# Loads that wait for their product of TensorE in the program, not in the plan alone

## The chip, the cores and the metric

The kernel runs on one core of a Trainium2 chip. The metric is the device time of one execution in microseconds (us); less is better. Engines are called as the profile calls them: PE (TensorE, matrix products), DVE (VectorE), ACT (ScalarE), POOL (GpSimd, which here only issues the row gathers), SP (SyncE, which here only issues loads and stores), and the 16 DMA engines that carry out what POOL and SP issue.

## The reference

Two branches work on the same x of 2048 tokens by 576, and a gate mixes them:

```python
g = sigmoid((x * gate_w).sum(-1))
a = irfft2(rfft2(x) * (w_r + 1j * w_i))          # branch A: a filter in the frequency domain
q = einsum("nd,dhc->nhc", x, w_q)                # branch B: 32 heads, two halves of 128 each
s1, s2 = q1 @ k1.T, q2 @ k2.T                    # 64 scores for each half
e = argmax(s1) * 64 + argmax(s2)                 # one expert of 4096 for each token and head
act = gelu(einsum("nd,nhd->nh", x, u[e]))
b = einsum("nh,nh,nhd->nd", softmax_over_one, act, v[e])
out = g * a + (1 - g) * b
```

All is float32. Every token reads 32 rows of u and v, 2 x 576 numbers each, from memory: 65,536 rows of 4,608 bytes, 302 MB in all.

## The kernel before, in words

The 2048 tokens are 16 tiles of 128. The 32 heads are 8 chunks (c = 0 to 7) of 4 heads. The work has two stages that overlap.

**Scores and experts (to about 585 us).** For each chunk, the key tables are first multiplied into the query weights: `build_m` takes five slices of w_q (i = 0 to 4, tiles `wqT` and `wq`, loaded by `load_wq` at L361 and L364 into a slot of the ring "uv") and makes a matrix of two parts, `mh` and `ml`. `scores(c, tp)` then multiplies two token tiles (tp = 0 to 7) with the five slices: a *score block*, written (c, tp) below, of ten jobs on PE (two tiles by five slices), 28 matmuls in all. The first job of a block, `score_jobs[c, tp][0]`, has three matmuls. DVE takes the maxima (`mx`, L446), ACT the signs (`sg`, L454), and a few operations later the experts' numbers stand in `ei`.

**Gathers and sums (all along, to the end).** `group(t, c)` fetches the rows of one token tile and one chunk: four gathers by POOL (L519), one a head, 128 rows of 4,608 bytes each, into slots of the ring "uv". DVE multiplies them with x and sums (L529), ACT applies the gelu (L533), and the second half of the row is added to the output, either by DVE (L561, or ACT L554 and DVE L555) or as a product with a diagonal matrix on PE (ACT makes `dg` at L571, PE accumulates, DVE adds at L587). Token tiles 0 to 9 are summed beside the scores; tiles 10 to 15 (`L_SEQ`) after them, and their x is loaded for this a second time (`xl`, by `load_xn`, L382).

**The frequency branch (from about 600 us).** `fold` adds and subtracts mirrored columns of x (DVE, L694 to L696) and PE multiplies with `kr`; `f2`, `f4`, `f6` and `invert` are products with tables: `fi` (loaded at L684), twiddle factors `tw` (L725) and the filter `w` (L732). `close_gates` makes the gate's sums from `xl` at L393.

**What sets the order.** Nothing is issued as it is written. Each operation is a job with an engine, a cost in us, a due time and the buffers it needs; `Plan.order` simulates engines, buffers and DMA by these costs and so fixes the order of the jobs on each engine and the buffer slots. The kernel then emits the jobs in that order. Along one engine a chain of dependencies without semaphores keeps the order (`after`, `on`). Between engines, semaphores come from the data alone: an instruction waits for what wrote its inputs and for what last used its buffer.

A job can also be given `after=[...]`: jobs that the plan lets end before it starts this one. It is a hint for the plan's clock. In the program it has no trace, unless the data ask for the same wait. Three kinds of loads have one:

- `load_wq` for slice i of chunk c+1: after the first job of the score block two before the block at which the slice is built (`BUILD`; none for the very first): 34 loads. The build itself is planned after the first job of the block just before.
- `load_xn` for the six `xl` tiles: after the first job of block (7, 7), the last.
- the load of `fi`: after the same job.

So 41 loads of the 120 DMAs that SP issues. (POOL's gathers have such an `after` too; the change does not touch them.)

The order of SP's queue around block (7, 7) is: `kr`, `gr`, `krb`, the six `xl`, `fi`, then the first `w` and `tw`, then the second `w` and `tw`, and so on. SP issues in order; one that waits holds all behind it.

Of the kernel before, what the change touches and what calls it, by code (L numbers as in the profile page):

```python
# [82 lines left out]


class Job:
    __slots__ = ("eng", "us", "at", "fn", "deps", "bufs", "move", "nr", "wait", "outs", "ready", "start", "end", "table")


REACH = {'POOL': 3.72, 'SP': 1.95}
# [167 lines left out]
def tile_kernel(ctx, tc, xn, xT, x5, wqT, wq5, kT, wri, uv, gw, t_kr, t_fi, t_tw, t_io, out):  # L257
# [13 lines left out]
    prev = {}  # L271

    def after(chain, i):
        if chain in prev:
            tc.add_manual_dep(
                i.ins, prev[chain].ins.name,
                mybir.DependencyInfo(mybir.DependencyClass.NoSync, mybir.DependencyReason.DATA),
                reason="order of the work")
        prev[chain] = i
# [19 lines left out]
    plan = Plan(sizes)  # L299
# [20 lines left out]
    def on(eng, i):  # L320
        after(eng, i)
# [8 lines left out]
    def ac(us, at, fn, w, r, **kw):  # L330
        return plan("ACT", us, at, lambda: on("ACT", fn()), w, r, **kw)

    def ld(us, at, fn, w, r=(), **kw):
        return plan("SP", 0.06, at, lambda: on("SP", fn()), w, r, move=us, **kw)

    vt, stt, actv = nc.vector.tensor_tensor, nc.vector.scalar_tensor_tensor, nc.scalar.activation
    pp = pools["pp"]
# [20 lines left out]
    def load_wq(c, i, at, after=()):  # L358
        w = wq_t[c, i] = buf("uv", ROW, view=lambda x: x.rearrange("p a d -> p (a d)")[:, : 8 * P].rearrange("p (g e) -> p g e", g=8))
        if i < 4:  # L360
            ld(load(P * 4096, 4096), at, lambda: nc.sync.dma_start(w.ap, wqT[c, i]), [w], after=after)  # L361
            return
        flat = lambda: w.ap.rearrange("p g e -> p (g e)")[:, 512:]
        ld(load(P * 2048, 2048), at, lambda: nc.sync.dma_start(flat(), wq5[c]), [w], after=after)  # L364
        ac(act(512), at + 2, lambda: actv(w.ap[:, :, :E], flat().rearrange("p (g e) -> p g e", e=E), AF.Copy), [w], [])
        ac(act(512), at + 2, lambda: actv(w.ap[:, :, E:], w.ap[:, :, :E], AF.Copy), [w], [])

    def load_x(b, i, at, at2, n=1):
        st = buf("uv", ROW, view=lambda x: x.rearrange("p a d -> p (a d)")[:, : n * 512])
        h = P if i < 4 else E  # L370
        src = lambda: xT[:, i, b * 512 : (b + n) * 512] if i < 4 else x5[:, b * 512 : (b + n) * 512]
        ld(load(h * n * 2048, n * 2048), at, lambda: nc.sync.dma_start(st.ap[:h], src()), [st])
        for m in range(n):
            hi = xts[i if i < 4 else 8][b + m]
            lo, r = (xts[4 + i][b + m], 0) if i < 4 else (hi, E)
            cut = lambda m=m: st.ap[:h, m * 512 : m * 512 + 512]
            ac(act(512), at2, lambda hi=hi, cut=cut: actv(hi.ap[:h], cut(), AF.Copy), [hi], [st])
            dv(dve(512), at2, lambda hi=hi, lo=lo, cut=cut: vt(lo.ap[r : r + h], cut(), hi.ap[:h].bitcast(F32), ALU.subtract), [lo], [st, hi])
# [245 lines left out]
    for s in range(NCH * 8):  # L624
        c, tp = divmod(s, 8)
        at = when(s)
# [17 lines left out]
        while todo and todo[0][0] * 8 / NE + LE <= s + 1:  # L644
            n, (t, cc) = todo[0]
            ready = t // 2 if cc == 0 and t // 2 < EARLY else t // 4 * 2 + 1
# [21 lines left out]
    def switch(m):  # L668
        sctx[m].close()
        pools[("la", "lb")[m]] = ctx.enter_context(  # L670
            tc.tile_pool(name=("la", "lb")[m], bufs=1, side=("right", "left")[m], reuse_waits="tile"))
# [223 lines left out]
    for n, t in enumerate(E_T + L_SEQ):  # L895
        at = inv0 + IPACE * n
# [5 lines left out]
    for n, (t, c) in enumerate(SEQ):  # L902
        at = TR + TGS * n
# [11 lines left out]
    for j in plan.order():  # L915
        for m in range(2):
            if not opened[m] and j.start >= plan.switch[m]:
                opened[m] = True
                switch(m)
        tc.cur_priority = int(j.start * 100) + 1000  # L920
        for b in j.bufs:
            if b.ap is None:
                b.ap = b.make(b.tag, b.slot)
        j.fn()


EARLY = 4
# [82 lines left out]
```

## Time and profile before

| | |
|---|---|
| time, median of 3 runs | 965.13 us (962.98 to 965.76) |
| the profiled execution: its own time | 973.46 us |
| its span, first to last instruction | 971.7 us |
| PE busy | 914.7 us (94%) |
| DVE busy | 878.6 us (90%) |
| ACT busy | 622.4 us (64%) |
| POOL busy | 566.0 us (58%) |
| DMA: the gathers' queue q0 | 302.02 MB, 82.0% of the 16 engines' span |
| DMA: SP's queue q1 | 41.94 MB, 11.8% |
| mean granted clock of PE | 0.984 |

How to read it: busy shares are means over the whole run, and two engines and the DMA are all above 90%. So what a change is worth can't be read from them; it is read from the stretch in which it acts, by what each engine waits for there. A profiled execution is one run, and this one was longer than the median of the timed ones; sums made from its rows are set against its own time.

### The profile page before, as it was taken

To read this page: it belongs to the slowest core of one execution; us is meant where nothing else is said; L and a number is where in the kernel's file an instruction comes from. 1 tells how busy PE (TensorE), PEld (TensorE's weight loads), DVE (VectorE), ACT (ScalarE), POOL (GpSimd) and SP (SyncE) were. 2 spreads that over 40 slices of the span, in tenths; PEclk is the share of its full clock that TensorE was granted. 3 is DMA by queue.
4 is the path that set the end of the run, shared out by engine and by line. 5 is a ranking of instruction groups with operands and counts; after the bars stand their busy time and mean duration, and the time that the engine had idled before them with its cause. 6 is when DMAs were issued, how large, how long until landed. Compare 5 with 4: busy or idle time off the path is not lost.

```text
span 971.7 us, 14880 instructions
## 1 busy us (share of the span) xinstructions
PE 914.7 (94%) x4288; PEld 747.3 (77%) x4288; DVE 878.6 (90%) x2030; ACT 622.4 (64%) x2211; POOL 566.0 (58%) x516
## 2 busy tenths in 40 slices
PE   7999999999999999999999993799999999999994
PEld 7888888788788888777878782787788787777763
DVE  3899989999999999999999889998999999967687
ACT  3987786977676776876788865664344444654443
POOL 0346666665565565565666656477674647756662
PEclk9999999999999999999999997899999999999997
DMA  9889999999998999899999998799998989999995
GB/s 325 276 283 406 356 327 371 318 378 362 343 356 334 342 379 342 318 372 379 333 350 378 389 420 325 298 347 413 418 385 331 401 292 390 378 391 379 409 367 238
DMA packets 90897, 344.90 MB, mean 355 GB/s; under 512 B 10240, under 2 KB 10752, under 8 KB 90816
## 3 DMA queue, kind: packets, MB, share of 16 engines
q0 software_dynamic: 73728, 302.02, 82.0%
q1 hardware_dynamic: 17088, 41.94, 11.8%
q8 instruction: 34, 0.56, 0.2%
q14 instruction: 47, 0.39, 0.1%
HBM read 339.20 MB, written 4.72 MB: 354 GB/s over the span
## 4 chain that ended last, share of the span: by engine, by line
PE 65%; DVE 16%; ACT 8%; issue 5%; DMA 4%; POOL 1%; another core or an unknown queue 0%; SPq 0%; DVEq 0%; POOLq 0%; ACTq 0%
PE p L318 65%; DVE uv L529 5%; DMA uv<-uv,ei 3%; ACT sg L454 3%; DVE xn L561 3%; DVE xn L555 2%; ACT uv L554 2%; DVE mx L446 1%; POOL uv L519 1%; ACT a L538 1%; ACT dg L571 1%; DMA uv<-wqT 1%; DVE t L753 0%; DVE t L752 0%; DVE sq L470 0%
## 5 line engine op out<-in xcount | busy, mean ns | idle before, releaser
L519 POOL DMA_INDIRECT uv<-uv,ei x512 | 565.8, 1105 | 389.2 <-PE p L318 110.4
L318 PE MATMUL p<-mh,xt 128*128 128x512 f32 x1152 | 383.6, 400 | 3.1 <-issue 1.7
L454 ACT ACTIVATE sg<-p,mx 128x64 bf16<-128x64 f32 x1024 | 231.3, 375 | 48.7 <-DVE mx L446 39.6
L318 PEld LDWEIGHTS p<-mh,xt 128*128 128x128 f32 x1152 | 216.5, 188 | 53.2 <-issue 1.9
L318 PE MATMUL p<-ml,xt 128*128 128x512 f32 x640 | 251.9, 394 | 0.0
L529 DVE SCALAR_TENSOR_TENSOR uv<-uv,xn 128x576 f32<-128x576 f32 x320 | 234.3, 749 | 6.6 <-DMA uv<-uv,ei 6.1
L318 PE MATMUL p<-uv,dg 128*128 128x288 f32 x800 | 209.8, 416 | 23.9 <-ACT dg L571 22.4
L318 PEld LDWEIGHTS p<-uv,dg 128*128 128x128 f32 x800 | 152.9, 194 | 70.7 <-ACT dg L571 26.8
L318 PEld LDWEIGHTS p<-ml,xt 128*128 128x128 f32 x640 | 120.4, 188 | 27.1
L529 DVE SCALAR_TENSOR_TENSOR uv<-uv,xl 128x576 f32<-128x576 f32 x192 | 138.6, 750 | 0.4 <-issue 0.3
L561 DVE SCALAR_TENSOR_TENSOR xn<-uv,a,xn 128x576 f32<-128x576 f32 x152 | 122.6, 809 | 0.9 <-issue 0.2
L533 ACT ACTIVATE b<-z 128x4 f32<-128x4 f32 x129 | 28.7, 223 | 141.0 <-DVE uv L529 103.7
L555 DVE TENSOR_TENSOR xn<-uv,xn 128x576 f32<-128x576 f32 x148 | 111.2, 752 | 3.1 <-ACT uv L554 1.3
L554 ACT ACTIVATE uv<-uv,a 128x576 f32<-128x576 f32 x148 | 104.7, 777 | 13.1 <-DVE a L542 9.8
L318 PE MATMUL p<-fi,bt 128*128 128x289 f32 x384 | 99.0, 411 | 3.6 <-DVE t L753 2.3
L318 PEld LDWEIGHTS p<-fi,bt 128*128 128x128 f32 x384 | 83.4, 243 | 17.0 <-issue 4.2
L318 PEld LDWEIGHTS p<-kT,uv 128*128 128x128 f32 x640 | 78.1, 195 | 8.8 <-issue 4.9
L318 PE MATMUL p<-kT,uv 128*128 128x128 f32 x640 | 78.9, 279 | 5.4 <-DMA uv<-wqT 4.9
L446 DVE TENSOR_REDUCE mx<-p 128x16 f32<-128x1024 f32 x64 | 77.8, 1216 | 6.1 <-PE p L318 6.0
L465 ACT ACTIVATE sg<-sg 128x256 bf16<-128x256 bf16 x192 | 79.2, 463 | 0.9
L571 ACT ACTIVATE dg<-ident,a 128x128 f32<-128x128 f32 x200 | 69.4, 409 | 2.5 <-PE p L318 2.4
L538 ACT ACTIVATE a<-b,sw 128x1 f32<-128x1 f32 x200 | 43.4, 305 | 1.0
(97 smaller groups left out, 708.4 us busy)
## 6 DMA issues: line engine op xcount, KB each, us to landing
uv<-wqT SPq DMA_DIRECT2D x32, 512.0 KB
uv<-uv,ei POOLq DMA_INDIRECT x512
w<-wri SPq DMA_DIRECT2D x16, 289.0 KB
out<-xn SPq DMA_DIRECT2D x16, 288.0 KB
xn<-xn SPq DMA_DIRECT2D x10, 288.0 KB
tw<-t_tw SPq DMA_DIRECT2D x9, 256.0 KB
uv<-xT SPq DMA_DIRECT2D x8, 256.0 KB
uv<-wq SPq DMA_DIRECT2D x8, 256.0 KB
```

The lines of the kernel that those rows point to most:

```text
L318: after("PE", nc.tensor.matmul(*args, **kw))
L446: dv(dve(1024, True), at + O_MAX, lambda: nc.vector.tensor_reduce(mv.ap[:, 2 * tp : 2 * tp + 2, :], ps.ap.rearrange("p a (g e) -> p a g e" ...
L454: on("ACT", actv(sg.ap[:, j, g, :], ps.ap[:, j, g * E : g * E + E], AF.Sign, bias=mv.ap[:, 2 * tp + j, g : g + 1], scale=-1.0))
L465: ac(act(256), at + O_ADD, lambda b=b: actv(s2()[:, :, b * Q : b * Q + Q], s2()[:, :, b * Q : b * Q + Q], AF.Copy, bias=b / 4), [sg], [])
L519: on("POOL", nc.gpsimd.indirect_dma_start(out=g.ap.rearrange("p a d -> p (a d)"), out_offset=None, in_=uv, in_offset=bass.IndirectOffsetOn ...
L529: dv(0.68, at + O_DOT, lambda k=k, g=rows[k]: stt(g.ap[:, 0, :], g.ap[:, 0, :], 1.0, x.ap, op0=ALU.mult, op1=ALU.mult, accum_out=z.ap[:, k ...
L533: ac(0.1, at + O_GELU, lambda: actv(b.ap[:, k0:k1], z.ap[:, k0:k1], AF.Gelu_apprx_tanh), [b], zk, table="gelu")
L538: on("ACT", actv(a.ap[:, k : k + 1], b.ap[:, k : k + 1], AF.Copy, scale=sw[:, t, c * HPC + k : c * HPC + k + 1]))
L554: ac(act(576), at + O_SCALE, lambda v=v, s=s: actv(v(), v(), AF.Copy, scale=s()), [(rows[k], 1)], [a])
L555: dv(dve(576), at + O_SUM, lambda v=v: vt(y.ap, v(), y.ap, ALU.add), [y], [(rows[k], 1)])
L561: dv(0.73, at + O_SUM, lambda v=v, s=s: stt(y.ap, v(), s(), y.ap, op0=ALU.mult, op1=ALU.add), [y], [(rows[k], 1), a])
L571: ac(0.3, at + O_DG, lambda k=k, dg=dg: actv(dg.ap, ident, AF.Copy, scale=a.ap[:, k : k + 1]), [dg], [a, "ident"])
```

## The change

Each load's `after` is now also put into the program. When a load is emitted, a dependency with a semaphore is added on the last instruction of each job that it names. To know that instruction, the last matmul of every PE job is kept in the job (`last`) when the job is emitted. The plan, its order on each engine and the buffer slots stay the same, and no DMA is added or taken away.

```diff
-    __slots__ = (..., "start", "end", "table")
+    __slots__ = (..., "start", "end", "table", "last")
...
-    def ld(us, at, fn, w, r=(), **kw):
-        return plan("SP", 0.06, at, lambda: on("SP", fn()), w, r, move=us, **kw)
+    def ld(us, at, fn, w, r=(), after=()):
+        def go():
+            i = fn()
+            on("SP", i)
+            for j in after:
+                tc.add_manual_dep(
+                    i.ins, j.last.ins.name,
+                    mybir.DependencyInfo(mybir.DependencyClass.Sync, mybir.DependencyReason.DATA),
+                    reason="not before its turn")
+
+        return plan("SP", 0.06, at, go, w, r, move=us, after=after)
...
         j.fn()
+        if j.eng == "PE":
+            j.last = prev["PE"]
```

More of the change, by code (lines that the diff above doesn't have):

```diff
@@ L85 @@
 class Job:
-    __slots__ = ("eng", "us", "at", "fn", "deps", "bufs", "move", "nr", "wait", "outs", "ready", "start", "end", "table")
+    __slots__ = ("eng", "us", "at", "fn", "deps", "bufs", "move", "nr", "wait", "outs", "ready", "start", "end", "table", "last")
 REACH = {'POOL': 3.72, 'SP': 1.95}
```

## The prediction

> **What bounds the kernel now.** I read the page first, then the busy time by stretches, the waits of TensorE (PE) by stretches, and the chain that ended last.
>
> ```profile
> span 971.7 us, 14880 instructions
> 540.00:560.00 20.00, 20.00 (x87) 15.93 (x85) 14.74 (x35) 16.31 (x75) 14.34 (x14) 1.00 1.01 385
> 560.00:580.00 20.00, 20.00 (x89) 16.37 (x88) 17.69 (x41) 11.49 (x46) 10.88 (x11) 1.00 1.03 420
> 580.00:600.00 20.00, 10.28 (x36) 7.42 (x34) 18.70 (x43) 12.84 (x58) 11.18 (x10) 0.83 0.85 329
> 600.00:620.00 20.00, 12.01 (x78) 11.58 (x79) 18.50 (x54) 11.49 (x36) 10.21 (x10) 0.74 0.95 370
> 620.00:640.00 20.00, 16.62 (x95) 14.51 (x94) 19.49 (x56) 14.16 (x55) 11.29 (x10) 0.91 0.72 238
> 640.00:660.00 20.00, 20.00 (x94) 17.36 (x93) 16.40 (x46) 13.15 (x33) 15.59 (x14) 1.00 1.00 391
> ```
>
> The columns after the length are PE, PE's weight loads, VectorE (DVE), ScalarE (ACT), GpSimd (POOL), PE's granted clock, the busy share of the DMA engines, GB/s. PE is full up to 580 and from 640. Between them it loses 21 us (60 less 10.28, 12.01 and 16.62), while DVE is nearly full. Just before, from 540 to 580, it is the other way round: the DMA engines are full (1.01, 1.03) and DVE has holes.
>
> The waits of PE, in the stretches 60 to 500 (three lines, all there are) and 577 to 640 (the two longest of four); the numbers are us in total, times, longest:
>
> ```profile
> PE p L318 <- ACT dg L571: 2.5, 2, 1.3
> PE p L318 <- issue: 1.7, 1, 1.7
> PE p L318 <- ACT sg L454: 1.1, 2, 0.8
> ...
> PE p L318 <- DVE f L695: 9.3, 3, 7.6
> PE p L318 <- ACT dg L571: 8.6, 2, 7.7
> ```
>
> Up to 500 PE hardly waits (5.3 us), so there only what makes PE itself late can cost. In 577 to 640 it waits 17.9 us for folds and diagonals that DVE and ACT deliver late. The chain that ended last tells why they are late:
>
> ```profile
> 490.70 6.72 DMA uv<-uv,ei
> ...
> 506.67 46.69 PE p L318 x196
> ...
> 559.21 14.40 DMA uv<-uv,ei
> ...
> 586.31 1.15 DVE mx L446
> ```
>
> PE carries the chain until 553; then a gather of rows that takes 14.40 us from issue to landing, where 6.72 was usual; then DVE, which works off what came late, reaches the row maxima (mx) at 586.31. ACT's signs and diagonals come behind these, and PE, whose row stands in the next fence, resumes at 592.14 behind the diagonals.
>
> **The change, part by part.** 41 loads carry an `after`: 34 of the key product's weights (L361, L364), six of x (xl, L382) and fi (L684). For each, SyncE (SP) now waits until the last matmul of the named score product is done. No transfer is added or removed; what moves is when SP issues, and what stands behind it in SP's queue.
>
> *The seven held behind the first product of the last score block, (7, 7).* Here are SP's issues, PE's matmuls, and the sizes:
>
> ```profile
> 526.55 27.10 SPq L382 DMA_DIRECT2D xl<-xn  x6
> 553.74 0.38 SPq L684 DMA_DIRECT2D fi<-t_fi  x1
> 554.17 0.42 SPq L732 DMA_DIRECT2D w<-wri  x1
> 554.65 0.42 SPq L725 DMA_DIRECT2D tw<-t_tw  x1
> ...
> 578.40 0.61 PE L318 MATMUL p<-mh,xt 128*128 128x512 f32 x2
> 584.07 0.39 PE L318 MATMUL p<-ml,xt 128*128 128x512 f32 x1
> 592.14 5.83 PE L318 MATMUL p<-uv,dg 128*128 128x288 f32 x16 [7.68 <-ACT dg L571]
> ...
> xl<-xn SPq DMA_DIRECT2D x6, 288.0 KB
> fi<-t_fi SPq DMA_DIRECT2D x1, 867.0 KB
> w<-wri SPq DMA_DIRECT2D x16, 289.0 KB
> tw<-t_tw SPq DMA_DIRECT2D x9, 256.0 KB
> ...
> q1 hardware_dynamic: 17088, 41.94, 11.8%
> ```
>
> The last score block ends with the matmul at 584.07. A block is 28 matmuls, some 0.23 us apart, so it begins 6.4 us before its end, and the first of the pair at 578.40 is the third matmul of its first product: done at about 578.8. Today the six xl loads go out from 526.55 to 553.65 and fi at 553.74. They will go out from 578.8 on: 25 to 52 us later. Behind them in SP's queue stand one load of w and one of tw (554.17, 554.65), which carry no `after` but move as well, by 24 us. In all 6 x 288 + 867 + 289 + 256 = 3140 KB, 3.2 MB. Queue q1 takes 11.8% of 971.7 us for 41.94 MB, 2.73 us for a MB: 8.8 us of all DMA engines leave the stretch 526 to 570, where the engines are full, and come back after 579.
>
> What it brings before 579 is bounded by what DVE loses there to late rows:
>
> ```profile
> DVE uv L529 <- DMA uv<-uv,ei: 3.7, 4, 1.4
> DVE mx L446 <- PE p L318: 2.5, 1, 2.5
> DVE uv L529 <- issue: 0.2, 1, 0.2
> ```
>
> These are all the waits of DVE from 553 to 577. The 2.5 us for PE stay, and come first, at 551 to 553; so DVE can gain 3.7 + 0.2 = 3.9 us behind them, and no more, though the rows may come 8.8 us sooner. I take 3.9 whole, because 8.8 is more than twice that. From 575 to 596 DVE has no hole, so it reaches mx at 582.4 in place of 586.31 (the scores that it reads are there at 578), ACT's diagonals follow, and PE resumes at 588.2: its wait of 7.68 becomes 3.8. PE is done with the scores at 584.5, so there is room for all 3.9. What is late next is the same as now, DVE's folds, 3.9 us earlier.
>
> What it costs after 579: 8.8 us of transfers beside the rows issued then. The stretch 580 to 640 has idle DMA time of 20 x (0.15 + 0.05 + 0.28) = 9.6 us to take them. The cover is that no wait of DVE for a DMA stands in 577 to 640; the longest of its two waits there is
>
> ```profile
> DVE xn L587 <- PE p L318: 1.7, 2, 1.3
> ```
>
> The held data themselves are wanted late:
>
> ```profile
> L393 DVE SCALAR_TENSOR_TENSOR p<-xl,gr x6: 758/760/767, 600.3 to 647.4; 128x576 f32<-128x576 f32 x6
> L726 ACT ACTIVATE tw<-tw x9: 292/309/313, 616.3 to 809.0; 128x128 f32<-128x128 f32 x9
> L318 PE MATMUL p<-fi,bt x384: 404/406/618, 650.8 to 938.5; 128*128 128x289 f32 x192
> ```
>
> The first xl at 600.3, tw at 616.3, fi at 650.8. Even at half speed, sharing with rows, all 3.2 MB are there at 578.8 + 2 x 8.8 + some 5 = 601, and the first xl long before. I cost the burst at nothing; uncovered it costs up to 8.8 us.
>
> [...]
>
> *The 34 weight loads.* I set each issue beside the end of its product. 17 go out after it already and do not move; 17 go out before it, by 0.3 to 8.7 us. One of the farther ones:
>
> ```profile
> 303.53 0.33 SPq L361 DMA_DIRECT2D uv<-wqT  x1
> ...
> 306.98 0.64 PE L318 MATMUL p<-mh,xt 128*128 128x512 f32 x2
> ...
> L318 PE MATMUL p<-kT,uv x16: 271/275/275, 317.0 to 318.7; 128*128 128x128 f32 x16
> ...
>   PE p L318: 4.9, 1
> ```
>
> The load goes at 303.53, its product ends at 307.4 (the first of the pair at 306.98), the build that reads it starts at 317.0: the lead falls from 13.5 to 9.6 us. It can't fall far below that in any of the 17, since the build stands behind the next block's first product. A transfer in this phase takes about the 6.72 us of the row gather above, so 2.9 us are left. The last line tells that PE waited for these loads once in the whole run, 4.9 us, at the start. Bounds of one load: below, a gain of its own 512 KB (1.4 us) for rows that now go first; above, 14.40 - 9.6 = 4.8 us, were it to take as long as the worst gather. I take 0, by the near row.
>
> *The semaphores themselves.* Up to 41 more waits on SP, which computes nothing and whose instructions cost other engines nothing, and an update at the end of a matmul. Matmuls release DVE all along (L587 above), and blocks that do so run at 0.23 us a matmul, so I take 0. The far end is a whole lost place of 0.23 us for each of the 28 products that are named (one by seven loads, seven by two): 6.4 us, which would leave a loss of 2.5.
>
> *Sum:* -3.9 us. Against the profiled execution's own 973.46: 969.6. That execution is 0.9% above the median of the runs, 965.13; scaled by 965.13/973.46 it gives **961.2 us**, 0.4% faster.
>
> **Rivals.**
> *Taken back.* DVE's 3.9 us turn into a wait elsewhere: the diagonals are held by ACT's own queue, or PE gains at 588 and waits longer at the folds, which already cost 9.3 us. For it: DVE and PE meet many times up to 640. Against it: DVE is nearly full from 580 to 640 and all of its work moves. Time: 965.1, no change.
>
> *Slower: the burst hits the rows.* At 578.8 nine loads leave within a few us. If rows that DVE needs at 585 to 597 are then late, DVE loses up to 8.8 and has won 3.9: +4.9, 978.4 on the profile's scale, 970.0 on the median's. It decides from the point where rows issued at 573 to 583 are used less than 8.8 us after they landed. For it: 559.21's 14.40 us came from just such a crowd. Against it: no row of 577 to 640 is waited for, and those rows will find less queue ahead of them.
>
> *Slower: a late build.* Two builds at 4.8 us each would make +9.6 - 3.9 = 5.7, 970.8. It needs transfers of over 9.6 us where 6.72 is usual.
>
> *More than forecast: the clock too.* PE's group at 592.14 took 5.83 us; the same 16 matmuls at full clock:
>
> ```profile
> 551.09 4.04 PE L318 MATMUL p<-uv,dg 128*128 128x288 f32 x16
> ```
>
> The granted clock of 580 to 600 is 0.83. If the shorter wait keeps it up, 1.8 us more are won, and DVE's wait of 1.3 us for that group goes: 3.9 + 1.8 + 1.3 = 7.0, 958.2. [...]
>
> **How the numbers follow.** Forecast 0.46 (its own range 959.5 to 963); more than forecast 0.08; taken back 0.28; the burst 0.12; late builds 0.06. About 0.3% (2.9 us) is what a measurement of this kernel can tell from no change. Faster is 0.54, same 0.28, slower 0.18. The range leaves the two slower cases out (the far end of the semaphores, 967.6, with them) and reaches from below the clock's case to a little over no change: 957.5 to 966.5.
>
> **What would show it.** SP issues xl, fi, w and tw at 579 or later; the row gather issued near 559 lands within 8 us; DVE has no wait for a DMA from 553 to 577; PE resumes the diagonals near 588; PE's loss from 580 to 640 falls from 21 to about 17 us; builds keep leads of over 9 us. The prediction is wrong if DVE waits for rows between 580 and 600, if PE's wait for the folds grows by what the diagonals won, or if a build waits for its weights.

## The result and the profile after

The changed kernel took 959.28 us (median of 5 runs, 958.75 to 960.32) and the kernel before, run beside it, 965.13 us (5 runs, 962.98 to 966.36): ratio 0.9942, 95% interval 0.9926 to 0.9957. It is 5.85 us faster, and the interval reaches from 4.2 to 7.1 us.

First, how to compare the profiles. The profile of before that the prediction reads was a long execution (span 971.7 us). A second profile of the same kernel is shorter, and it is the fairer partner; it is called *before, second profile* here. In the changed kernel the code below the edit stands nine lines lower or a little more (L382 is L391, L529 is L538, L446 is L455, L571 is L580). The heads of the two pages, changed kernel first:

```profile
span 957.1 us, 14883 instructions
...
PE 912.7 (95%) x4288; PEld 747.7 (78%) x4288; DVE 877.6 (92%) x2030; ACT 623.0 (65%) x2211; POOL 566.6 (59%) x516
```

```profile
span 963.0 us, 14880 instructions
```

The work is the same, since DVE is busy for 877.6 us where the page of before has 878.6. What is gone is idle time. SP's queue in the changed kernel (start, us, operation):

```profile
575.56 3.00 SPq L391 DMA_DIRECT2D xl<-xn  x6
578.61 0.43 SPq L693 DMA_DIRECT2D fi<-t_fi  x1
579.08 0.43 SPq L741 DMA_DIRECT2D w<-wri  x1
582.21 0.33 SPq L734 DMA_DIRECT2D tw<-t_tw  x1
```

The six loads of xl now leave within 3.00 us, where the issues took 27.10; fi and w go right behind them, and tw 2.7 us after w. (w and tw carry no `after` and yet leave 28.6 and 31.2 us later than in the second profile of before, at 550.53 and 551.01 there: they stand behind the loads that wait. The score block itself ends 3 us earlier in this profile than in the one that the prediction reads, so 575.56 is the predicted place.) The gathers issued from 555 to 575 (count, median us from issue to landing), and DVE's waits for rows from 545 to 577 (us in total, times, longest), changed kernel first:

```profile
uv<-uv,ei POOLq DMA_INDIRECT x13, 6.9
...
DVE uv L538 <- DMA uv<-uv,ei: 0.2, 1, 0.2
```

Before, second profile:

```profile
uv<-uv,ei POOLq DMA_INDIRECT x11, 12.2
...
DVE uv L529 <- DMA uv<-uv,ei: 5.0, 7, 1.4
```

In these 20 us SP's queue moves 2.17 MB in the second profile of before (27.1% of the 16 engines) and nothing in the changed kernel. Without these bytes beside them rows land in 6.9 us and not in 12.2, and DVE's wait for rows falls from 5.0 us to 0.2. Now the same instructions further on: DVE's factors at 490, the row maxima of the last block, PE's diagonals and first fold, DVE's sum behind the diagonals. Before, second profile:

```profile
490.64 0.16 DVE L542 SCALAR_TENSOR_TENSOR a<-b,sw 128x4 f32<-128x4 f32 x1 [0.49 <-ACT b L533]
589.80 1.23 DVE L446 TENSOR_REDUCE mx<-p 128x16 f32<-128x1024 f32 x1
590.51 5.73 PE L318 MATMUL p<-uv,dg 128*128 128x288 f32 x16 [7.18 <-ACT dg L571]
596.28 0.76 DVE L587 TENSOR_TENSOR xn<-p,xn 128x576 f32<-128x576 f32 x1 [1.21 <-PE p L318]
603.88 2.47 PE L318 MATMUL p<-kr,f 128*128 128x128 f32 x10 [7.64 <-DVE f L695]
```

The changed kernel:

```profile
488.51 0.16 DVE L551 SCALAR_TENSOR_TENSOR a<-b,sw 128x4 f32<-128x4 f32 x1 [0.38 <-ACT b L542]
583.65 1.21 DVE L455 TENSOR_REDUCE mx<-p 128x16 f32<-128x1024 f32 x1
584.35 4.15 PE L318 MATMUL p<-uv,dg 128*128 128x288 f32 x16 [3.16 <-ACT dg L580]
588.83 0.75 DVE L596 TENSOR_TENSOR xn<-p,xn 128x576 f32<-128x576 f32 x1
596.40 2.48 PE L318 MATMUL p<-kr,f 128*128 128x128 f32 x10 [7.90 <-DVE f L704]
```

Read the differences down the list: 2.13 us at 490, 6.15 at the maxima, 7.45 at the sum behind the diagonals, 7.48 at the first fold. The 2.13 us are there long before any of the seven loads. Most of them arise near 430, where PE waits 2.04 us in the second profile of before and 1.70 in the changed kernel, and runs at half clock (0.50 in 429.91 to 433.32) afterwards in the first alone (see the last section). The seven profiles of the changed kernel and of e1, e2 and e4 to e7 stand at 487.86 to 488.92 here, the three of the kernel before (two, and e8) at 490.64 to 491.78; e2 and e5 are among the seven and are not faster than before. So the 2.13 us are not counted as the change's gain; whether they are chance is not shown. Then the stretch gives 4.0 us (6.15 less 2.13), and the diagonals 1.3 more (7.45 less 6.15): their wait is shorter by 4.0 us (7.18 to 3.16), they ran at full clock (4.15 us in place of 5.73), and DVE's wait of 1.21 us for them went. 4.0 + 1.3 = 5.3 us is inside the measured interval.

The other profiles bear this out. From DVE's factors at 490 to the first fold it takes 107.9 us in the changed kernel, in e1 and in e6, and 109.2 in e7; in the three profiles of the kernel before and in e2, e4 and e5 it takes 112.4 to 114.4. Behind the first fold a part goes again: the spans 963.0 and 957.1 differ by 5.9 us only, since the rest takes 359.1 us before and 360.7 here. The held loads are not the reason, since e1 has them and takes 359.1 too.

The stretches after, to set against those in the prediction:

```profile
560.00:580.00 20.00, 20.00 (x89) 16.45 (x88) 19.86 (x46) 12.45 (x48) 16.04 (x14) 1.00 1.00 392
580.00:600.00 20.00, 7.93 (x33) 5.94 (x31) 20.00 (x50) 15.22 (x62) 11.97 (x11) 0.83 1.03 417
600.00:620.00 20.00, 15.42 (x100) 14.71 (x100) 18.45 (x55) 12.83 (x44) 8.12 (x8) 0.83 0.95 364
620.00:640.00 20.00, 19.78 (x108) 16.60 (x109) 19.50 (x58) 14.45 (x50) 13.59 (x13) 1.00 0.84 296
```

The holes of DVE in 560 to 580 are closed (19.86). The DMA engines are full in 580 to 600 (1.03, it was 0.85) because the burst lies there (SP's queue takes 42.1% of them), and DVE is still full beside it (20.00). PE loses 16.9 us in 580 to 640.

### The profile page after: what moved, and what is told of

Same layout as the page of the kernel before. It is cut to its first block, busy times and chain, and to the rows that moved or that the text cites. A ratio compares the mean times of both kernels' runs of the same rounds, so it can differ in the third digit from the quotient of the medians.

```text
span 957.1 us, 14883 instructions
## 1 busy us (share of the span) xinstructions
PE 912.7 (95%) x4288; PEld 747.7 (78%) x4288; DVE 877.6 (92%) x2030; ACT 623.0 (65%) x2211; POOL 566.6 (59%) x516
## 4 chain that ended last, share of the span: by engine, by line
PE 68%; DVE 22%; ACT 4%; issue 3%; DMA 1%; SPq 0%; DVEq 0%; ACTq 0%
PE p L318 68%; DVE uv L538 8%; DVE xn L570 4%; DVE xn L564 3%; ACT sg L463 2%; DVE mx L455 1%; ACT uv L563 1%; DMA uv<-uv,ei 1%; DVE t L762 1%; DVE sq L479 1%; DVE t L761 1%; DVE im L490 0%; ACT a L547 0%; DMA uv<-wqT 0%; DVE bt L827 0%
## 5 line engine op out<-in xcount | busy, mean ns | idle before, releaser
L538 DVE SCALAR_TENSOR_TENSOR uv<-uv,xn 128x576 f32<-128x576 f32 x320 | 234.4, 751 | 2.0 <-DMA uv<-uv,ei 1.3
L318 PEld LDWEIGHTS p<-ml,xt 128*128 128x128 f32 x640 | 120.4, 188 | 27.1
L538 DVE SCALAR_TENSOR_TENSOR uv<-uv,xl 128x576 f32<-128x576 f32 x192 | 138.7, 751 | 0.3 <-issue 0.3
L542 ACT ACTIVATE b<-z 128x4 f32<-128x4 f32 x129 | 28.6, 222 | 140.8 <-DVE uv L538 140.3
L455 DVE TENSOR_REDUCE mx<-p 128x16 f32<-128x1024 f32 x64 | 77.9, 1218 | 4.5 <-PE p L318 4.4
L580 ACT ACTIVATE dg<-ident,a 128x128 f32<-128x128 f32 x200 | 69.8, 410 | 2.9 <-PE p L318 2.8
```

Source lines behind the costliest of these rows:

```text
L318: after("PE", nc.tensor.matmul(*args, **kw))
L455: dv(dve(1024, True), at + O_MAX, lambda: nc.vector.tensor_reduce(mv.ap[:, 2 * tp : 2 * tp + 2, :], ps.ap.rearrange("p a (g e) -> p a g e" ...
L538: dv(0.68, at + O_DOT, lambda k=k, g=rows[k]: stt(g.ap[:, 0, :], g.ap[:, 0, :], 1.0, x.ap, op0=ALU.mult, op1=ALU.mult, accum_out=z.ap[:, k ...
L542: ac(0.1, at + O_GELU, lambda: actv(b.ap[:, k0:k1], z.ap[:, k0:k1], AF.Gelu_apprx_tanh), [b], zk, table="gelu")
L580: ac(0.3, at + O_DG, lambda k=k, dg=dg: actv(dg.ap, ident, AF.Copy, scale=a.ap[:, k : k + 1]), [dg], [a, "ident"])
```

## Experiments

Ratios are to the kernel before, run in turn with each experiment. Three chips were used: one for e1 to e4, one for e5 to e8, one for e9 to e12. Theory A throughout is that the gain comes from the later issue of the seven loads.

**e1, the seven loads alone.** The 34 weight loads no longer wait:

```
-    def ld(us, at, fn, w, r=(), after=()):
+    def ld(us, at, fn, w, r=(), after=(), sem=True):
...
-            for j in after:
+            for j in after if sem else ():
...
(in load_wq, both loads)
-... after=after)
+... after=after, sem=False)
```

> Only the six xl loads and fi wait in the program; the 34 weight loads go as before. Theory A (the gain comes from the 3.2 MB that leave the full stretch 526 to 570): nearly all of the change's 5.85 us, 4 to 6 us faster than before; DVE waits for rows under 0.5 us in all just ahead of the end of the scores, PE's wait for the diagonals falls from 7.7 to some 3 to 4 us. Theory B (the weight loads carry a good part, since in the profile of the changed kernel PE is already 3.3 us ahead at 270): 2 to 3 us faster here. Theory C (chance of a few us between executions): within 1 us of before.

960.81 us, ratio 0.9955 (0.9941 to 0.9970). DVE has no wait for a DMA from 545 to 577, and the diagonals are those of the changed kernel:

```profile
584.10 4.15 PE L318 MATMUL p<-uv,dg 128*128 128x288 f32 x16 [3.15 <-ACT dg L580]
```

**e2, the weight loads alone.** As e1, but `sem=False` on the loads of xl and fi in place of those in load_wq.

> Only the 34 weight loads wait; the six xl loads and fi go as before. Theory A: within 1.5 us of before, and the gather beside the early xl and fi loads still takes 12 to 15 us from issue to landing. Theory B: 2 to 3.5 us faster, with PE about 3 us ahead at 270 in every profile. Theory C: no change, with the 3 us at 270 sometimes there and sometimes not.

966.32 us, ratio 1.0006 (0.9994 to 1.0018). Rows issued from 555 to 575 still take 11.0 us (median). The wait for rows and the late diagonals at half clock are as before:

```profile
DVE uv L538 <- DMA uv<-uv,ei: 6.4, 8, 1.4
...
488.92 0.16 DVE L551 SCALAR_TENSOR_TENSOR a<-b,sw 128x4 f32<-128x4 f32 x1 [1.12 <-ACT b L542]
589.36 6.38 PE L318 MATMUL p<-uv,dg 128*128 128x288 f32 x16 [7.76 <-ACT dg L580]
```

So the gain is that of the seven loads, and for the 34 others none is seen either way. The middle line also shows why the 2.13 us at 490 are not counted: e2 is 1.72 us early there too, and has 1.15 left at the diagonals (589.36 against 590.51).

**e3, the kernel before again.** No edit.

> The kernel before, unchanged, to see how far its profiled executions differ among themselves. All theories: ratio 1.000, within 0.2%. Theories A and C: its profile is some 965 us long rather than 971.7, and PE's two stalls of 1.2 and 1.3 us at 187 and 267 may be missing. Theory B: the stalls are there again.

966.24 us, ratio 1.0003 (0.9989 to 1.0018). This gave the second profile of before that is used above. PE is busy all of 180 to 280 in it (100.00 us); in the first one it is idle for 2.56 us there, in two stalls.

**e4, fi alone.** As e1, and `sem=False` on xl too; w and tw stand behind fi in SP's queue and move with it.

> Only fi waits (and with it the first w and tw, which stand behind it in SP's queue); the six xl loads and the weight loads go as before. Of the 3.2 MB 1.45 MB leave the stretch, 45%. Theory A: 2 to 4 us faster than before, and the worst gather of 545 to 575 takes 9 to 11 us in place of 14.4. Theory B and C: within 1.5 us of before.

962.75 us, ratio 0.9968 (0.9954 to 0.9983), about half of the gain. Gathers issued from 555 to 575 land as fast as in the changed kernel, but DVE had already waited for earlier ones, beside xl (issued from 522.63 to 547.03):

```profile
uv<-uv,ei POOLq DMA_INDIRECT x11, 7.1
...
DVE uv L538 <- DMA uv<-uv,ei: 5.9, 5, 1.5
...
487.86 0.16 DVE L551 SCALAR_TENSOR_TENSOR a<-b,sw 128x4 f32<-128x4 f32 x1 [0.79 <-ACT b L542]
587.47 5.95 PE L318 MATMUL p<-uv,dg 128*128 128x288 f32 x16 [6.93 <-ACT dg L580]
```

By the time, part of the bytes taken away gives part of the gain. The profile does not show where: DVE's wait of 5.9 us is no less than the 5.0 of before, and of the 3.04 us by which the diagonals come sooner, 2.78 were there at 490 already.

**e5, the same semaphores on an earlier product.** The seven wait for the first product of (7, 4); the order stays that of the changed kernel:

```
-            for j in after:
+            for j in after if sem is None else sem:
...
-        load_xn(t, "xl", T0 - 19 + n, score_jobs[NCH - 1, XL[n]][:1])
+        load_xn(t, "xl", T0 - 19 + n, score_jobs[NCH - 1, XL[n]][:1], sem=score_jobs[NCH - 1, 4][:1])
(and fi in the same way)
```

> The changed kernel, the seven loads (six xl, fi) waiting by the same semaphores, but for the first product of (7,4) in place of (7,7): it ends near 556, in the stretch in which VectorE waits for gathers, so the 3.2 MB start there and not behind it. The order is that of the changed kernel. Theory A (the gain comes of the time at which the seven loads go, behind the stretch): the gain is gone, 964 to 969 us, VectorE's wait for uv by DMA in 545 to 577 at 4 us or more, and the diagonals at 128x288 late and at half clock again (5.7 us or more for 16). Theory D (any wait that keeps these loads from running ahead, or any delay of 5 to 30 us, is enough): 959 to 961 us, no wait of VectorE for DMA.

965.36 us, ratio 0.9995 (0.9982 to 1.0008): the gain is gone. SP's first issue, the gathers of 555 to 575, DVE's three long waits for rows behind 573, and the diagonals:

```profile
552.59 2.70 SPq L391 DMA_DIRECT2D xl<-xn  x6
...
uv<-uv,ei POOLq DMA_INDIRECT x12, 14.2
...
573.16 0.76 DVE L538 SCALAR_TENSOR_TENSOR uv<-uv,xn 128x576 f32<-128x576 f32 x1 [1.10 <-DMA uv<-uv,ei]
575.81 0.76 DVE L538 SCALAR_TENSOR_TENSOR uv<-uv,xn 128x576 f32<-128x576 f32 x1 [1.14 <-DMA uv<-uv,ei]
577.91 0.76 DVE L538 SCALAR_TENSOR_TENSOR uv<-uv,xn 128x576 f32<-128x576 f32 x1 [0.57 <-DMA uv<-uv,ei]
...
587.73 6.79 PE L318 MATMUL p<-uv,dg 128*128 128x288 f32 x16 [6.54 <-ACT dg L580]
```

Up to 572 this kernel was where the changed one is, within 0.3 us. Then the burst, 23 us earlier than there, met rows that are wanted soon after they land; they took 14.2 us, DVE lost 2.8 us in these three waits, and PE's group fell back to half clock. So the wait as such gains nothing, and where the burst comes decides. The expected 4 us of DVE's waits in 545 to 577 were only 2.5, since the last of the three lies behind 577:

```profile
DVE uv L538 <- DMA uv<-uv,ei: 2.5, 3, 1.1
```

**e6, the burst twice.** The changed kernel with the seven pieces moved once more, meant to go behind fi:

```
+    def load_fi():
+        i = nc.sync.dma_start(fi.ap, t_fi)
+        for n, t in enumerate(L_SEQ):
+            nc.sync.dma_start(scr[n], xn[t])
+        nc.sync.dma_start(scf, t_fi)
+        return i
```

> The changed kernel, and behind fi on the same queue the same seven pieces are moved once more, from their sources to a place in DRAM that nothing reads: 3.2 MB more behind the product, nothing in front of it. Theory A with the burst hidden (rows issued in 585 to 603 were used 10 to 17 us after they had landed): most of the additional 8.8 us of DMA is covered too, 959 to 963 us, VectorE's wait for uv by DMA in 580 to 640 below 2 us. The rival of the prediction (the burst hits rows): each microsecond of DMA counts, 964 to 970 us, and VectorE's waits for uv by DMA in that window 4 us or more.

961.55 us, ratio 0.9953 (0.9933 to 0.9973). It did not do what it was meant to. Only the load of fi itself waits for the product, and the copies, which depend on nothing, were issued at the start:

```profile
26.63 7.63 SPq L699 DMA_DIRECT2D scr<-xn  x6
34.73 0.49 SPq L700 DMA_DIRECT2D scf<-t_fi  x1
...
575.84 3.09 SPq L391 DMA_DIRECT2D xl<-xn  x6
```

So nothing follows for a doubled burst. That the burst of 3.2 MB is hidden rests on the changed kernel's own waits.

**e7, the clock held for the folds.** PE multiplies kr by kr ahead of its first fold:

```
+            for i in range(warm.pop() if warm else 0):
+                mm(pf[:, :P], kr.ap, kr.ap, start=True, stop=True)
             for i in range(ND):
```

with `warm = [24]`.

> The changed kernel with 24 more matmuls of 128x128 (kr by kr, into a part of the fold's PSUM tile that the fold overwrites) ahead of the first fold on TensorE: at 0.25 us each, 6 of the 7.90 us in which it waits there for VectorE. If the granted clock falls for what idles before (half from 593.3 for 10.2 us in the changed kernel), it stays full there: the first fold's five products take 1.3 us and not 2.48, the next ones follow as fast as VectorE brings f, and the time falls by 1 to 3 us to 956 to 958. If the clock falls for something else (power, the engine's load), or if VectorE sets the pace of the folds: 959 to 960, no change.

960.06 us, ratio 0.9931 (0.9914 to 0.9949), which cannot be told from the changed kernel's. The filling ended 2.16 us too early: the clock, full (1.00) in 595.49 to 598.90 with PE busy for 1.25 us of it, was at half (0.50) in 598.90 to 602.31. Another thing was seen by chance: the diagonals came behind the same 3.16 us of waiting as in the changed kernel, and ran at half clock all the same.

```profile
584.01 1.22 DVE L455 TENSOR_REDUCE mx<-p 128x16 f32<-128x1024 f32 x1
...
584.71 5.84 PE L318 MATMUL p<-uv,dg 128*128 128x288 f32 x16 [3.16 <-ACT dg L580]
...
598.06 1.71 PE L318 MATMUL p<-kr,f 128*128 128x128 f32 x10 [2.16 <-DVE fe L493]
...
590.59 0.76 DVE L596 TENSOR_TENSOR xn<-p,xn 128x576 f32<-128x576 f32 x1 [1.32 <-PE p L318]
```

DVE waited 1.32 us for them and reached its sum at 590.59, not 588.83: 1.76 us later than in the changed kernel. Of these 0.36 us were there at the maxima (584.01 against 583.65), so 1.4 us arise here. This is the price of the clock at this one place.

**e8, the clock held in the kernel before.** 20 such matmuls ahead of the diagonals, written to columns of the PSUM tile that nothing reads; no load is moved.

> The kernel before, with 20 more matmuls of 128x128 (kr by kr, into columns of the PSUM tile that nothing reads) on TensorE between the last product and the first diagonals: 5 us of the 7.2 us that TensorE waits there. No load is moved. This takes the clock's part of the gain by itself: the 16 diagonals take 4.15 us in place of 5.73. Theory A (wait 4.0 to 4.5 and clock 1.6 of the 5.85 us): faster than before by 1.6 us, 964 to 965. If the clock's part is not worth anything by itself (the folds behind wait for VectorE in any case): 966, no change.

965.6 us, ratio 0.9991 (0.9975 to 1.0006). The diagonals ran at full clock behind a real wait of 3.35 us:

```profile
591.56 4.15 PE L318 MATMUL p<-uv,dg 128*128 128x288 f32 x16 [3.35 <-ACT dg L575]
```

The 1.6 us that were expected are not shown: the interval allows from 2.4 us faster to 0.6 slower. At DVE the most there was to win was its wait of 1.21 us. In the trace it is won: from the maxima (590.85) to the sum behind the diagonals (596.03) DVE takes 5.18 us, as in the changed kernel, and 6.48 in the second profile of before.

**e9, e10, e11: the clock held in the changed kernel**, with 12 matmuls ahead of the diagonals, 32 ahead of the first fold and 8 ahead of the ninth (e9), the 32 alone (e10), the 12 alone (e11); and **e12, the changed kernel again**, without an edit.

> The changed kernel with matmuls of 128x128 (kr by kr, results that nothing reads) in three of TensorE's gaps: 12 ahead of the diagonals (gap 3.15 us; 0.23 us each, 2.8 us), 32 ahead of the first fold (gap 7.90 us; 7.4 us; the 24 of the run before ended 2.16 us ahead of it and the clock fell all the same), 8 ahead of the ninth fold (gap 2.17 us; 1.8 us). In the traces so far a slice of 3.41 us with 2.04 us or more of idle TensorE in it is followed by half clock, one with 1.88 or less is not. If that holds: no half clock from 580 to 640, 16 diagonals in 4.15 us and the first fold in 1.3 in every execution, and 956 to 958.5 us against the changed kernel on the same chip (959.3). If VectorE sets the folds' pace in any case: as the changed kernel, within 1 us.

> The changed kernel with the 32 matmuls ahead of the first fold alone. If the half clock of 593 to 603 costs anything on the path: 957 to 958.5. If VectorE sets the pace there: 959 to 960.

> The changed kernel with the 12 matmuls ahead of the diagonals alone. There the changed kernel's own gap of 3.15 us left the clock full in some profiles and halved it for 3.41 us in one (585.25), where VectorE then waited 1.3 us for the diagonals. If the place of the gap against the clock's slices decides by chance from run to run: 958 to 959.3, up to 1 us below the changed kernel, and less spread. If not: as the changed kernel.

> The changed kernel again, unaltered, for the other three on the same chip: 958.5 to 960.5 us, ratio 0.993 to 0.996 to the kernel before. Its diagonals come near 584.4 behind a gap of 3.1 to 3.2 us, in 4.15 us where the gap straddles two of the clock's slices (at most 1.9 us in either) and in 5.8 us where one slice holds 2.0 us or more of it.

On this third chip every kernel was slower and spread more (before: 979.21 us, 974.21 to 986.32 over 35 runs), so every time that was expected was missed. The ratios come from runs taken in turn and are not the quotients of these medians.

| kernel | median | ratio | 95% interval |
|---|---|---|---|
| e12, changed | 978.53 us | 0.9972 | 0.9942 to 1.0002 |
| e9, all three gaps | 979.1 us | 0.9983 | 0.9952 to 1.0014 |
| e11, diagonals | 977.89 us | 0.9992 | 0.9968 to 1.0015 |
| e10, first fold | 982.88 us | 1.0035 | 1.0010 to 1.0061 |

For e12 958.5 to 960.5 was expected; its gain of 0.28% is half of the first one, with an interval that just holds no change. Its diagonals, expected near 584.4 behind 3.1 to 3.2 us, came at 592.82 behind 5.02 us and at half clock; those of e11, with the 12 matmuls ahead, at full (4.15 us) behind 2.32.

```profile
592.82 5.75 PE L318 MATMUL p<-uv,dg 128*128 128x288 f32 x16 [5.02 <-ACT dg L580]
```

The clock did what was expected in e9 up to 607. PE, its busy time behind the length, kept the full clock (1.00), and the first fold took 1.35 us:

```profile
580.00:607.32 27.32, 22.21 (x145) 19.66 (x143) 27.32 (x66) 16.48 (x66) 17.65 (x17) 1.00 1.01 398
607.32:614.15 6.83, 3.16 (x15) 3.16 (x16) 2.08 (x7) 1.52 (x6) 3.18 (x4) 0.50 1.03 420
...
603.86 1.35 PE L318 MATMUL p<-kr,f 128*128 128x128 f32 x10 [0.66 <-DVE f L713]
610.99 7.34 PE L318 MATMUL p<-kr,f 128*128 128x128 f32 x50 [5.78 <-ACT f L712]
```

No gain over e12 is seen: PE then waited 5.78 us, and in the 6.83 us from 607.32 DVE was busy for only 2.08. A stop of PE, ACT and DVE together, at 606 to 615, stands in the profiles of e9, e10 and e12, and not in that of e11 nor on the other chips. In these records some DMA completions are missing, and what the engines waited for is not named. The DMA engines are full there (1.03 in the line from 607.32), so rows that come late behind the burst, the danger that the prediction named, are a candidate; it was not tested, and the kernel before left no profile on this chip. So what stopped them, why e10 is slower than e12, and how much the change is worth on this chip stay open. No version here is shown to beat the changed kernel.

## Why the prediction was right

Forecast 961.2 us (its own sum gives 961.26; range 957.5 to 966.5); measured 959.28. The mechanism came as written, and one term was too small.

- *SP issues the seven and what stands behind them with the last block.* Yes: 575.56 to 582.21, right behind the first product of a block that ends 3 us sooner.
- *The bytes leave, rows land in 8 us.* Yes: 6.9 us median in place of 12.2, DVE's wait for rows 0.2 us. So the traces decide for the later issue, and e5 shows that the place counts: at 552.59 it gains nothing (0.9995), at 575.56 it does (0.9942).
- *The term -3.9.* Its size was read as DVE's waits in 553 to 577, and 4.0 is what the stretch gave between the two nearer profiles (6.15 at the maxima less 2.13 that were there before). PE's wait came to 3.16 us, where 3.8 was forecast; that is 4.02 less than in the second profile of before. That 3.9 and 4.0 agree so closely is partly luck: the 3.9 was read in one long execution, and the second profile of before has 4.4 us of waits for rows in the same stretch, 553 to 577.
- *The clock, set at nothing and left to a rival at 0.08.* This is the term that was mis-sized. What the clock grants behind the 3.8 us of waiting that were forecast no run shows. With 3.16 us it held: 16 diagonals in 4.15 us and no wait of DVE behind them, 1.3 us more, the price that e7 puts at 1.4. Of the rival's 1.8 and 1.3 only one counts, because what reaches the folds is DVE's delay and not PE's. And it is not settled by the length of the wait alone: the same 3.16 us gave half clock in e7. By timing it isn't shown, since e8, which takes it alone, can't be told from no change.
- *The burst at nothing.* In the changed kernel DVE has no wait for a DMA from 577 to 640, although the engines are at 1.03 in 580 to 600. The rival was a real danger: in e5 the same burst, where rows are wanted soon, cost what had been won. On the third chip it stays open.
- *Weight loads and semaphores at nothing.* e2 measured both together, 34 of the 41 added waits on SP among them: 1.0006 (0.9994 to 1.0018). So their far ends, 9.6 and 6.4 us, are out, and what such waits cost the other engines is less than this run can tell. In the changed kernel too PE waits for these loads only once, 4.9 us at the start.
- *Taken back.* PE's wait for the folds did not grow by what the diagonals won (7.64 to 7.90); the first fold is 7.48 us earlier.

## What to carry to other kernels

A load that is issued long before its use was not free here, where another engine waited for transfers beside it: the seven went out 46 us and more before their first use, the rows beside them took 12.2 us (6.9 without them), and DVE waited 5.0 us for rows (0.2 without them). So look at how long the transfers take that another engine waits for, and hold such a load back to a point behind which rows have slack, not merely later (e5 with 0.9995 against the changed kernel with 0.9942). Do one part of the change alone early: here seven of 41 loads carry the whole gain. And check in the trace that an added transfer went where the experiment wanted it; e6 did not.

## What the runs showed of the hardware

In these traces the clock did not follow the length of PE's gap but its place against slices of 3.41 us. In the changed kernel the granted clock falls to half at 593.32, is full again from 603.56, half from 613.80 and full from 617.22: 10.24, 10.24 and 3.41 us lie between, three slices, three and one. Stretches cut in steps of 3.41 us (counted back from 593.32 in the changed kernel, and from 585.25, where a half clock begins, in e7), from the changed kernel and then from e7; the first number behind the length is PE's busy time, and the third from the end is the clock:

```profile
579.67:583.08 3.41, 1.52 (x7) 0.94 (x5) 3.41 (x11) 3.39 (x19) 0.91 (x1) 1.00 1.04 419
583.08:586.49 3.41, 2.14 (x9) 1.72 (x10) 3.41 (x8) 3.41 (x16) 0.63 (x1) 1.00 1.04 418
...
593.32:596.73 3.41, 0.33 (x1) 0.36 (x2) 3.41 (x13) 1.25 (x5) 2.52 (x3) 0.50 1.03 417
```

```profile
581.84:585.25 3.41, 0.54 (x2) 0.49 (x3) 3.41 (x11) 3.41 (x19) 0.00 (x0) 1.00 1.04 417
585.25:588.66 3.41, 3.41 (x8) 2.36 (x7) 3.41 (x10) 3.41 (x17) 1.07 (x1) 0.50 1.03 414
```

In the changed kernel the gap of 3.16 us is split between two slices (1.52 and 2.14 us busy are left in them) and the clock stays full; in e7 nearly all of it lies in one slice (0.54 busy), and the next slice runs at half. In the second profile of before a gap of only 2.04 us did the same:

```profile
426.49:429.91 3.42, 1.38 (x8) 1.02 (x8) 3.42 (x10) 3.42 (x19) 2.23 (x3) 1.00 0.98 341
429.91:433.32 3.41, 3.41 (x10) 2.65 (x9) 3.41 (x9) 2.12 (x8) 1.42 (x2) 0.50 0.99 379
```

Of the slices at full clock, one with 2.04 us idle (1.38 busy) was followed by half clock, and one with 1.89 idle (1.52 busy) was not. That the idle time of one slice sets the clock of the next is the author's reading of them; what lies between 1.89 and 2.04 is not shown. A slice at half clock was followed by another with less: in the changed kernel PE is idle for 1.01 us of 596.73 to 600.15, and the half clock lasts to 603.56. So what e9 says of 1.88 us or less holds of slices at full clock alone. The start of the run tells nothing: in the changed kernel PE is idle up to its first matmul at 4.90 us, and the trace's first record of the clock begins at 9.64.

The kernel before took 966.07, 965.62 and 979.21 us on the three chips of the experiments. The change was worth 0.58% when it was first measured; on these chips its seven loads alone gave 0.45% on the first (e1), the changed kernel with copies early on 0.47% on the second (e6), and the changed kernel itself 0.28% on the third, with an interval that holds zero.
